# Packed attention values in one 128-column matmul per key chunk and head pair, in place of two of 64 columns

## The chip, the cores and the metric

The kernel runs on one core of one Trainium2 chip. The metric is the device time of one execution in microseconds (us). Three runs of the kernel before took 1108.59, 1109.92 and 1108.97 us, median 1108.97 us. A profile of one execution is read beside them.

TensorE is called PE below, and its loading of the stationary operand PEld; VectorE is DVE, ScalarE is ACT, GpSimd is POOL, and SyncE, which issues the transfers, is SP.

## The reference

Four batches, eight heads, 576 tokens, head dimension 64, 32 packed queries `p` per head. Two attentions follow each other, and two feed-forward stages follow them:

```python
def sm_attn(qq, kk, vv):
    s = scale * qq @ kk.T
    a = exp(s - max(s)); a = a / (sum(a) + 1e-9)
    return a @ vv
p_packed = sm_attn(p, k, v)            # 32 x 64 per head
out = sm_attn(q, p_packed, p_packed)   # 576 x 64 per head
# x: 2304 x 512; four experts of width 1024 with relu, weighted by domain_probs
# then h = x @ w_in (512 x 2048); g = h - tanh(h); g @ w_out
```

The change is in `a @ vv` of the first attention: 32 packed queries times 576 keys times 64 value columns, for 32 pairs of batch and head.

## The kernel before

The first attention is done per batch `b` and per half `g` of its eight heads. A half is two head pairs `jj`, a pair is two heads `h` whose value columns lie side by side. `pack_T(b, g)` transposes the softmax weights on PE into `a1t` (four chunks of 128 keys, for each of them 128 weight columns: two pairs, two heads, 32 queries) and `a1e` (the last 64 keys). `pack_pv(b, g)` multiplies them with the values: the value columns `vt` are the stationary operand, the weight columns stream. Per pair, per key chunk `c` (five, of which the last has 64 keys) and per head there is one matmul with 64 value columns and 32 weight columns. Head 0 writes PSUM partitions 0 to 63, head 1 partitions 64 to 127. The fp32 matmuls of this kind are two records each in the trace, a load and a stream each. At the end ACT copies the partitions 0 to 63 and DVE those from 64 to 127 into `ppbd`, block-diagonal, from which the second attention (`q_scores`, tile `qsc`) and the folded first expert weights (`pack_w1`, tile `wps`) read.

The order of the start is written out as a string of tokens. P is `pack_pv`, T is `pack_T`, M, E and N are the packed scores, their exponentials and their normalisation, Q, R and X are the scores, the normalisation and the transposes of the second attention, W is `pack_w1`, u and d are the expert's first and second matmuls (tiles `hps` and `yps`), f are filling matmuls on zeros (tile `warm`). `pack_pv` stands eight times there: P00 P01, one behind the other, in START_A, P02 and P03 in START_M, P10 to P13 in START_B. The two digits count groups of two batches and the four halves in each. PE runs in this written order from the start to the end of the expert stage. DVE and ACT follow it as far as START_M; in START_B and later the scheduler orders them by its own forecast, and by it the scheduler also chooses which of the four PSUM buffers of the pool `ps1` (tag p1: tp, te, pv, qsc, qtp, yps) a tile takes, and so whose release its first matmul waits for. The last stage (`h3ps`, `ops`) is ordered by the scheduler on all engines.

Of the kernel before, what the change touches and what calls it, by code (L numbers as in the profile page):

```python
# [8 lines left out]
F32 = mybir.dt.float32  # L9
F32R = mybir.dt.float32r  # L10
U32 = mybir.dt.uint32
ACTF = mybir.ActivationFunctionType
# [44 lines left out]
def kernel(  # L57
# [13 lines left out]
    nc = tc.nc  # L71
# [5 lines left out]
    def pool(name, bufs=1, stack=None, **kw):  # L77
        return (stack or ctx).enter_context(
            tc.tile_pool(name=name, bufs=bufs, **kw, **({} if kw.get('space') == DRAM else {'reuse_waits': 'tile'}))
        )  # L80
# [15 lines left out]
    ps1 = pool("ps1", 4, space=PSUM)  # L96
# [22 lines left out]
    ppbd, a2h, a2l = {}, {}, {}  # L119
# [7 lines left out]
    kv_k, kv_v, qs = {}, {}, {}  # L127
# [84 lines left out]
    def pack_pv(b, g):  # L212
        a1t, a1e = a1ts.pop((b, g))
        bi = b % 2
        pv = ps1.tile([128, 2, 32], F32, tag="p1", name="pv")
        for jj in range(2):
            j = 2 * g + jj
            for c in range(5):
                n = 128 if c < 4 else 64
                for h in range(2):  # L220
                    k0 = 64 * jj + 32 * h
                    nc.tensor.matmul(  # L222
                        out=pv[64 * h:64 * h + 64, jj, :],
                        lhsT=kv_v[b][c][0:n, 128 * j + 64 * h:128 * j + 64 * h + 64],
                        rhs=a1t[:, c, k0:k0 + 32] if c < 4 else a1e[0:64, k0:k0 + 32],
                        start=(c == 0), stop=(c == 4),
                    )
        js = slice(2 * g, 2 * g + 2)
        nc.scalar.activation(out=ppbd[b // 2][0:64, bi, js, 0:32], in_=pv[0:64], func=ACTF.Copy)
        nc.vector.tensor_copy(out=ppbd[b // 2][64:128, bi, js, 32:64], in_=pv[64:128])  # L230

    def q_scores(p, t0):
        nt = min(2, TP - t0)
# [249 lines left out]
    def late_norm():  # L483
# [8 lines left out]
        "R": lambda p, i: q_norm(p, 2 * i),  # L492
        "T": lambda p, i: pack_T(2 * p + i // 2, i % 2),
        "P": lambda p, i: pack_pv(2 * p + i // 2, i % 2),
        "Z": pp_split,
        "I": pp_init,
# [243 lines left out]
```

## Time and profile before

| what | value |
|---|---|
| three runs | 1108.59, 1109.92, 1108.97 us, median 1108.97 |
| profiled execution, its own time | 1108.61 us |
| its span, first to last instruction | 1106.8 us |
| granted clock of TensorE over the span | 1.00, the level of 2.4 GHz |
| PE busy | 1095.2 us, 99% of the span |
| PE records of `pack_pv` | 320 loads and 320 streams, between 12.6 and 84.5 us |

The page gives busy times and the chain of waits that ended last. The timeline gives starts. A PE record's duration is modelled and overlaps the next one, so what a matmul costs is read from one start to the next. The clock was 1.00 in every stretch that is used here.

### The profile page before, as it was taken

Reading aid. Unit: us, or ns where it says so; the run is one execution under the profiler, and the core shown is the slowest. Engines: PE = TensorE matmul, PEld = TensorE weight load, DVE = VectorE, ACT = ScalarE, POOL = GpSimd, SP = SyncE. Lnnn points to the kernel's source line nnn. Section 1 sums busy time; section 2 is a strip of 40 time slices with the busy share of each in tenths; the row PEclk is TensorE's granted clock in tenths of the full one; section 3 lists DMA queues with packets and bytes.
Section 4 is the critical chain, followed back from the end, with each engine's and each line's share of the span. In section 5 each row is a group of like instructions: output and inputs, shape, how many; then the busy total and the mean of one; then the engine's idle time right before and its main releaser. Section 6 shows DMA issues by size and latency. Waiting matters only on the chain.

```text
span 1106.8 us, 15428 instructions
## 1 busy us (share of the span) xinstructions
PE 1095.2 (99%) x6476; PEld 915.9 (83%) x6476; DVE 711.3 (64%) x960; ACT 468.5 (42%) x661; POOL 7.2 (1%) x11
## 2 busy tenths in 40 slices
PE   8999999999999999999999999999999999999998
PEld 6787888898888888888888888888888888888887
DVE  4636446776676676676676434587676757777775
ACT  3434433232332332333233112466657656656463
POOL 0100000000000000000000000000000000000000
PEclk9999999999999999999999999999999999999999
DMA  9731113223232241241331040401001262202102
GB/s 332 238 89 40 38 41 113 93 82 111 96 115 94 78 151 65 89 141 69 95 115 57 20 153 1 152 1 38 9 30 39 86 219 95 77 1 76 63 14 77
DMA packets 33669, 96.72 MB, mean 87 GB/s; under 512 B 3776, under 2 KB 3776, under 8 KB 33600
## 3 DMA queue, kind: packets, MB, share of 16 engines
q1 hardware_dynamic: 33600, 95.73, 25.3%
q8 instruction: 51, 0.84, 0.3%
q14 instruction: 18, 0.15, 0.0%
HBM read 69.51 MB, written 26.21 MB: 86 GB/s over the span
## 4 chain that ended last, share of the span: by engine, by line
PE 97%; DVE 1%; ACT 1%; DMA 0%; issue 0%; DVEq 0%; SPq 0%; ACTq 0%
PE yps L412 36%; PE hps L386 18%; PE ops L652 18%; PE h3ps L596 18%; PE wps L361 3%; PE pv L222 1%; PE qsc L244 1%; PE xps L447 1%; PE sc L166 1%; DMA kt<-in_kT_dram 0%; PE qtp L283 0%; PE tp L204 0%; ACT a L180 0%; DVE mx L175 0%; DVE a L191 0%
## 5 line engine op out<-in xcount | busy, mean ns | idle before, releaser
L412 PE MATMUL yps<-w2h,hm 128*128 128x512 f32 x640 | 208.9, 394 | 0.0
L596 PE MATMUL h3ps<-xh,ws 128*128 128x512 f32 (+1 forms) x640 | 187.2, 369 | 0.0
L652 PE MATMUL ops<-ws,gh 128*128 128x512 f32 x576 | 178.4, 396 | 0.0
L412 PE MATMUL yps<-w2h,hu 128*128 128x512 f32 x512 | 166.6, 391 | 0.0
L423 DVE SCALAR_TENSOR_TENSOR x<-yps,pn,x 128x512 f32<-128x512 f32 x126 | 94.6, 751 | 100.4 <-PE yps L412 97.9
L386 PE MATMUL hps<-a2h,wph 128*128 128x256 f32 (+1 forms) x512 | 152.3, 297 | 1.8 <-DVE xl L453 0.9
L386 PE MATMUL hps<-a2h,wpl 128*128 128x256 f32 (+1 forms) x512 | 151.8, 297 | 0.7 <-DVE wpl L368 0.7
L386 PE MATMUL hps<-a2l,wph 128*128 128x256 f32 (+1 forms) x512 | 151.7, 296 | 0.3 <-DVE a2l L287 0.3
L412 PEld LDWEIGHTS yps<-w2h,hm 128*128 128x128 f32 x640 | 120.3, 188 | 37.1 <-issue 12.6
L596 PEld LDWEIGHTS h3ps<-xh,ws 128*128 128x128 f32 x640 | 116.5, 189 | 20.5
L652 PEld LDWEIGHTS ops<-ws,gh 128*128 128x128 f32 x576 | 107.7, 189 | 24.0 <-ACT gh L631 0.2
L412 PE MATMUL yps<-w2l,hm 128*128 128x512 f32 x320 | 125.2, 391 | 0.0
L596 PE MATMUL h3ps<-xl,ws 128*128 128x512 f32 (+1 forms) x320 | 117.9, 368 | 0.0
L412 PEld LDWEIGHTS yps<-w2h,hu 128*128 128x128 f32 x512 | 96.3, 188 | 20.2 <-PE wps L361 0.8
L652 PE MATMUL ops<-ws,gl 128*128 128x512 f32 x288 | 110.9, 395 | 0.0
L395 ACT ACTIVATE hu<-hps 128x512 fp32r<-128x512 f32 x64 | 38.3, 598 | 168.5 <-PE hps L386 168.4
L395 ACT ACTIVATE hm<-hps 128x640 fp32r<-128x640 f32 x64 | 45.1, 704 | 135.4 <-PE hps L386 135.4
L386 PEld LDWEIGHTS hps<-a2h,wph 128*128 128x128 f32 x512 | 97.1, 190 | 5.5 <-DVE xl L453 1.1
L412 PE MATMUL yps<-w2l,hu 128*128 128x512 f32 x256 | 100.1, 391 | 0.0
L386 PEld LDWEIGHTS hps<-a2l,wph 128*128 128x128 f32 x512 | 97.2, 190 | 2.8 <-DVE a2l L287 0.5
L386 PEld LDWEIGHTS hps<-a2h,wpl 128*128 128x128 f32 x512 | 97.1, 190 | 0.9 <-DVE wpl L368 0.9
L396 DVE SCALAR_TENSOR_TENSOR hm<-hps,hm 128x640 fp32r<-128x640 f32 x64 | 52.7, 824 | 58.2 <-ACT hm L395 57.3
(95 smaller groups left out, 1402.2 us busy)
## 6 DMA issues: line engine op xcount, KB each, us to landing
w1f<-in_w_dram SPq DMA_DIRECT2D x16, 512.0 KB, 5.0
st<-in_w_dram SPq DMA_DIRECT2D x16, 512.0 KB, 3.8
f<-in_win_dram SPq DMA_DIRECT2D x16, 512.0 KB, 3.5
f<-in_wout_dram SPq DMA_DIRECT2D x16, 512.0 KB, 3.5
win<-fo SPq DMA_DIRECT2D x16, 512.0 KB, 2.6
wout<-fo SPq DMA_DIRECT2D x16, 512.0 KB, 2.6
ws<-win SPq DMA_DIRECT2D x16, 512.0 KB, 4.9
ws<-wout SPq DMA_DIRECT2D x16, 512.0 KB, 5.4
```

What stands on the lines that cost most here:

```text
L166: nc.tensor.matmul(out=sc[64 * jj:64 * jj + 64, h, 0:288], lhsT=pbd[:, 4 * b + j, :], rhs=kv_k[b][j][:, 288 * h:288 * h + 288],)
L222: nc.tensor.matmul(out=pv[64 * h:64 * h + 64, jj, :], lhsT=kv_v[b][c][0:n, 128 * j + 64 * h:128 * j + 64 * h + 64], rhs=a1t[:, c, k0:k0 + ...
L244: nc.tensor.matmul(out=sc[r - r0:r - r0 + 64, 256 * i:256 * i + 256].rearrange("p (r j k) -> p r j k", r=2, j=4)[:, :, j, :], lhsT=qs[2 * ...
L361: nc.tensor.matmul(out=ps[32 * j:32 * j + 32, r, :], lhsT=ppbd[p][d, bi, j, 32 * r:32 * r + 32], rhs=w1f[c, j // 2][d, j % 2, :],)
L386: nc.tensor.matmul(out=ps[:, ff, 0:n], lhsT=a[c, p, bi][:, g, c0:c0 + 128], rhs=x[p][:, g, t0:t0 + n], start=(k == 0), stop=(k == 5),)
L395: last[1] = nc.scalar.activation(out=hi[:, :, d], in_=ps[:, :, 0:n], func=ACTF.Relu).ins
L396: last[0] = nc.vector.scalar_tensor_tensor(out=lo[:, :, d], in0=ps[:, :, 0:n], scalar=0.0, in1=f(hi[:, :, d]), op0=ALU.max, op1=ALU.subtra ...
L412: nc.tensor.matmul(out=ps, lhsT=a[:, ff, o:o + 128], rhs=w[c, fp][:, ff], start=(k == 0), stop=(k == 11),)
L423: last[0] = nc.vector.scalar_tensor_tensor(out=x2[tt], in0=ps, scalar=pn[:, tt, e:e + 1], in1=x2[tt], op0=ALU.mult, op1=ALU.add,).ins
L447: nc.tensor.transpose(ps[:, k, 128 * i:128 * i + 128], x2[t0 + i][:, c0:c0 + 128], ident)
L596: nc.tensor.matmul(out=ps[:, ff, 0:n], lhsT=w[:, wl, kd, :], rhs=x[:, kd, :], start=(k == 0), stop=(k == 11),)
L652: nc.tensor.matmul(out=ops[u][t], lhsT=a[ff][:, d], rhs=w[:, wl], start=(i == 0 and ff == 0 and k == 0), stop=(i == 3 and ff == 1 and k == 2),
```

## The change

Per pair and key chunk there is one matmul in place of two: all 128 value columns of the pair are stationary, and the 64 weight columns of both heads stream. The output is 128 partitions by 64 columns, of which the two diagonal blocks are what is wanted: head 0 in partitions 0 to 63 and columns 0 to 31, head 1 in partitions 64 to 127 and columns 32 to 63. The off-diagonal blocks are not read. Tile `pv` becomes twice as wide, and the two copies at the end read a column slice of it.

```diff
-        pv = ps1.tile([128, 2, 32], F32, tag="p1", name="pv")
+        pv = ps1.tile([128, 2, 64], F32, tag="p1", name="pv")
...
-                for h in range(2):
-                    k0 = 64 * jj + 32 * h
-                    nc.tensor.matmul(
-                        out=pv[64 * h:64 * h + 64, jj, :],
-                        lhsT=kv_v[b][c][0:n, 128 * j + 64 * h:128 * j + 64 * h + 64],
-                        rhs=a1t[:, c, k0:k0 + 32] if c < 4 else a1e[0:64, k0:k0 + 32],
-                        start=(c == 0), stop=(c == 4),
-                    )
+                k = slice(64 * jj, 64 * jj + 64)
+                nc.tensor.matmul(
+                    out=pv[:, jj, :],
+                    lhsT=kv_v[b][c][0:n, 128 * j:128 * j + 128],
+                    rhs=a1t[:, c, k] if c < 4 else a1e[0:64, k],
+                    start=(c == 0), stop=(c == 4),
+                )
...
-        nc.scalar.activation(out=ppbd[b // 2][0:64, bi, js, 0:32], in_=pv[0:64], func=ACTF.Copy)
-        nc.vector.tensor_copy(out=ppbd[b // 2][64:128, bi, js, 32:64], in_=pv[64:128])
+        nc.scalar.activation(out=ppbd[b // 2][0:64, bi, js, 0:32], in_=pv[0:64, :, 0:32], func=ACTF.Copy)
+        nc.vector.tensor_copy(out=ppbd[b // 2][64:128, bi, js, 32:64], in_=pv[64:128, :, 32:64])
```

The file is one line shorter: what was line 222 is 221 now, and later lines move up by one too.

On PE, at P01 (two pairs) and the first scores of the second attention behind it, before:

```order
L222 MATMUL pv<-a1t,vt 64x32 x8
L222 MATMUL pv<-a1e,vt 64x32 x2
L222 MATMUL pv<-a1t,vt 64x32 x8
L222 MATMUL pv<-a1e,vt 64x32 x2
L244 MATMUL qsc<-ppbd,qt 64x2x32 x32
```

and after:

```order
L221 MATMUL pv<-a1t,vt 128x64 x4
L221 MATMUL pv<-a1e,vt 128x64
L221 MATMUL pv<-a1t,vt 128x64 x4
L221 MATMUL pv<-a1e,vt 128x64
L243 MATMUL qsc<-ppbd,qt 64x2x32 x32
```

The place in the order is the same; ten matmuls of full width stand for twenty of half width. So it is at all eight calls.

On ACT in START_B, where Q04, Q03, S10 (a packed score with its softmax), X02 and d000, d001 stand in the written order, before:

```order
L260 ACTIVATE a_624<-a_624 128x512 [waits DVE_49]
L421 ACTIVATE x_683<-yps,pn 128x512 [waits DVE_49,PE_49,Activation_49]
L286 ACTIVATE a2h<-qtp 128x2x256 [waits PE_49]
L260 ACTIVATE a_696<-a_696 128x256 [waits DVE_49,Activation_49]
L260 ACTIVATE a_723<-a_723 128x512 [waits DMAHW5_49,DVE_49]
L180 ACTIVATE a_740,ss<-sc,nm 128x576 [waits DMAHW1_49,DVE_49]
```

and after:

```order
L259 ACTIVATE a_584<-a_584 128x512 [waits DVE_49]
L285 ACTIVATE a2h<-qtp 128x2x256 [waits PE_49]
L420 ACTIVATE x_643<-yps,pn 128x512 [waits DVE_49,Activation_49]
L180 ACTIVATE a_700,ss<-sc,nm 128x576 [waits DMAHW1_49,DVE_49]
L259 ACTIVATE a_656<-a_656 128x256 [waits DVE_49,Activation_49]
L259 ACTIVATE a_683<-a_683 128x512 [waits DMAHW5_49,DVE_49]
```

The copy of d000's result (`x<-yps`) now stands behind the copy of X02's transposes (`a2h<-qtp`), and the exponential of S10 ahead of the two of Q04 and Q03.

On DVE at the same place, before:

```order
L267 TENSOR_SCALAR qsm<-qsm 128x16 [waits DVE_49]
L270 RECIPROCAL qsm<-qsm 128x16 [waits DVE_49]
L271 TENSOR_TENSOR a_624<-a_624,qsm 128x512 [waits DVE_49]
L254 TENSOR_REDUCE qmx<-qsc 128x8 [waits PE_49]
L254 TENSOR_REDUCE qmx<-qsc 128x16 [waits PE_49]
L175 TENSOR_REDUCE mx<-sc 128x1 [waits PE_49]
L257 TENSOR_TENSOR a_696<-qsc,qmx 128x256 [waits DVE_49]
L257 TENSOR_TENSOR a_723<-qsc,qmx 128x512 [waits DMAHW5_49,DVE_49]
L177 TENSOR_SCALAR nm<-mx 128x1 [waits DVE_49]
L287 TENSOR_TENSOR a2l<-qtp,a2h 128x2x256 [waits Activation_49]
```

and after:

```order
L253 TENSOR_REDUCE qmx<-qsc 128x8 [waits PE_49]
L266 TENSOR_SCALAR qsm<-qsm 128x16 [waits DVE_49]
L269 RECIPROCAL qsm<-qsm 128x16 [waits DVE_49]
L253 TENSOR_REDUCE qmx<-qsc 128x16 [waits PE_49]
L270 TENSOR_TENSOR a_584<-a_584,qsm 128x512 [waits DVE_49]
L175 TENSOR_REDUCE mx<-sc 128x1 [waits PE_49]
L177 TENSOR_SCALAR nm<-mx 128x1 [waits DVE_49]
L286 TENSOR_TENSOR a2l<-qtp,a2h 128x2x256 [waits Activation_49]
L256 TENSOR_TENSOR a_656<-qsc,qmx 128x256
L256 TENSOR_TENSOR a_683<-qsc,qmx 128x512 [waits DMAHW5_49]
```

Both maxima of Q04 and Q03 now stand ahead of the normalisation of R02 (`a<-a,qsm`), which X02 transposes, and X02's remainder (`a2l`) ahead of the two subtractions. With this order d001's `yps` got another PSUM buffer. Its first matmul waited for ACT, for the copy of d000's result (`x<-yps`); now it waits for DVE, for `a2l<-qtp`, the last reader of X02's transposes. On PE, after:

```order
L282 MATMUL qtp<-ident,a_584 128x128 [waits DVE_49,PE_49,Activation_49]
L282 MATMUL qtp<-ident,a_584 128x128 x3
L411 MATMUL yps<-w2h,hu 128x512 [waits DVE_49]
```

X02's four transposes and d001's first matmul follow each other on PE in both kernels; only what the last row waits for has changed. The last stage is shuffled too on PE, ACT and DVE, with the same instructions.

## Rows read from the trace of the kernel before

**Rows 1.** The page's first part: busy us (share of the span), instructions.

```profile
PE 1095.2 (99%) x6476; PEld 915.9 (83%) x6476; DVE 711.3 (64%) x960; ACT 468.5 (42%) x661; POOL 7.2 (1%) x11
```

**Rows 2.** Windows: stretch, us, busy PE, PEld, DVE, ACT, POOL, clock, DMA.

```profile
36.00:106.00 70.00, 69.96 (x726) 55.82 (x725) 38.14 (x84) 28.05 (x54) 2.35 (x1) 1.00 0.40 128
...
720.00:1060.00 340.00, 340.00 (x1547) 280.79 (x1546) 246.08 (x250) 206.72 (x254) 0.00 (x0) 1.00 0.18 61
```

**Rows 3.** Chain that ended last, to 180 us: start us, us, what.

```profile
12.69 3.32 PE pv L222 x80
...
82.92 1.65 PE pv L222 x40
```

**Rows 4.** Lines 222 and 481: operation, count, duration ns minimum/median/maximum, starts, forms.

```profile
L222 PEld LDWEIGHTS pv<-a1t,vt x256: 132/138/139, 12.6 to 84.1; 128*64 128x64 f32 x128
...
L481 PEld LDWEIGHTS warm<-blank x56: 186/192/334, 1.0 to 34.7; 128*128 128x128 f32 x56
```

**Rows 5.** Timeline of PE at P00 and P01: start us, us, what, count.

```profile
12.42 0.27 PE L205 MATMUL te<-ident,a 128*64 128x128 f32 x1
12.62 0.66 PE L222 MATMUL pv<-a1t,vt 128*64 128x32 f32 x16
...
15.91 0.45 PE L244 MATMUL qsc<-ppbd,qt 128*64 128x64 f32 x8
```

**Rows 6.** Timeline of PEld, P00's first pair and the next pair's start.

```profile
12.62 0.55 PEld L222 LDWEIGHTS pv<-a1t,vt 128*64 128x64 f32 x16 [0.20 <-issue]
13.21 0.19 PEld L222 LDWEIGHTS pv<-a1e,vt 64*64 64x64 f32 x4
13.44 0.55 PEld L222 LDWEIGHTS pv<-a1t,vt 128*64 128x64 f32 x16
```

**Rows 7.** Timeline of PEld: loads of 128 columns behind each other.

```profile
8.88 1.19 PEld L481 LDWEIGHTS warm<-blank 128*128 128x128 f32 x10 [0.44 <-issue]
...
54.61 0.19 PEld L412 LDWEIGHTS yps<-w2h,hm 128*128 128x128 f32 x1 [0.44 <-ACT a2h L286]
54.72 0.19 PEld L412 LDWEIGHTS yps<-w2l,hm 128*128 128x128 f32 x1
```

**Rows 8.** Timelines of PE and PEld: a transpose and filling matmuls behind it.

```profile
34.41 0.27 PE L205 MATMUL te<-ident,a 128*64 128x128 f32 x1
...
34.41 0.53 PEld L481 LDWEIGHTS warm<-blank 128*128 128x128 f32 x4
```

**Rows 9.** Timeline of PE ahead of P13.

```profile
82.30 0.39 PE L412 MATMUL yps<-w2l,hm 128*128 128x512 f32 x1
82.53 0.39 PE L412 MATMUL yps<-w2h,hm 128*128 128x512 f32 x1
82.85 0.54 PE L222 MATMUL pv<-a1t,vt 128*64 128x32 f32 x12
```

**Rows 10.** Timeline of PE behind P02: X01's transposes, T03, P03.

```profile
32.07 0.66 PE L283 MATMUL qtp<-ident,a 128*128 128x128 f32 x4
...
33.95 0.63 PE L204 MATMUL tp<-ident,a 128*128 128x128 f32 x4 [1.22 <-DVE a L191]
...
35.26 0.66 PE L222 MATMUL pv<-a1t,vt 128*64 128x32 f32 x16
```

**Rows 11.** Timeline of all engines around X02 and d001.

```profile
44.26 0.69 DVE L271 TENSOR_TENSOR a<-a,qsm 128x512 f32<-128x512 f32 x1
44.87 1.01 DVE L254 TENSOR_REDUCE qmx<-qsc 128x8 f32<-128x256 f32 x2
...
45.98 0.66 PE L283 MATMUL qtp<-ident,a 128*128 128x128 f32 x4
...
46.39 0.48 PE L412 MATMUL yps<-w2h,hu 128*128 128x512 f32 x1
...
46.67 0.60 ACT L286 ACTIVATE a2h<-qtp 128x512 fp32r<-128x512 f32 x1 [2.01 <-PE qtp L283]
...
47.75 0.68 DVE L287 TENSOR_TENSOR a2l<-qtp,a2h 128x512 fp32r<-128x512 f32 x1
```

## The prediction

> **What bounds the kernel now.** I read the page's first part: PE is busy 99% of the span [rows 1]. So what matters is PE's own time, and where PE still waits. The windows say that it waits almost nowhere: from 36 to 106 us it is busy for 69.96 of 70.00 us, in the last stage for 340.00 of 340.00 [rows 2]. The chain of waits that ended last shows where the eight calls of `pack_pv` lie on the way to the end: the pieces named pv begin with P00 and P01, 3.32 us, and end with P13, 1.65 us [rows 3]; between them stand P03, P10, P11 and P12 with 1.72, 1.65, 1.65 and 1.65 us. Seven of eight calls are on the chain. P02 alone is not, since PE sits idle for 1.22 us behind it [rows 10]. So 14 of the 16 head pairs cost what they take, in full, and nothing behind P03 absorbs it.
>
> **What a pair costs before.** The timeline of PE gives four pairs from 12.62 to 15.91 us [rows 5]: 0.823 us each. The loads show what is inside [rows 6]. Sixteen loads of the four full chunks take 0.55 us with a last one of 0.138 [rows 4]: the two heads load and stream side by side, in opposite halves of the array, and a step of such two is (0.55 - 0.138) / 7 = 0.059 us. There are ten steps per pair, because each fp32 matmul is two records. From the last step of the full chunks (12.62 + 0.55 - 0.138 = 13.03) to the first load of the chunk of 64 keys at 13.21 [rows 6] it is 0.18 us, and from its last step (13.21 + 0.19 - 0.131 = 13.27) back to 128 rows at 13.44 it is 0.17. Each change of shape thus costs some 0.11 to 0.12 us beyond a step, during which the array runs empty.
>
> So half of the records go, but they ran two at a time. The count of matmuls is no measure of the gain; the length of a step is.
>
> **What a pair costs after.** A step is now one load of 128 columns and one stream of 64. The nearest rows for the load: two loads of 128 columns behind each other, with nothing to stream in between, start at 54.61 and 54.72; ten filling loads take 1.19 us with a last one of 0.192, (1.19 - 0.192) / 9 = 0.111 [rows 7]. The durations agree: 192 ns for 128 columns and 138 for 64 [rows 4], 54 ns more for 64 columns more. I take 0.110 per step. The stream does not matter: the filling matmuls stream 128 columns in 0.111 [rows 7], so 64 need at most 0.056 and lie under the next load.
>
> The Trainium skill says the same of the load ("TensorE: Matmul & The Clock Gate", LDWEIGHTS): its time goes by the columns, columns over 1.2 in ns, so 107 ns for 128 and 53 for 64, whatever the rows. This speaks against the change, and the 54 ns between the two durations [rows 4] agree; by the page's 107 the sum below would be 14 x 8 x 0.003 = 0.3 us lower.
>
> The change between 128 and 64 rows stays, as the fifth chunk still has 64 keys. Its waits grow by the longer load (0.054) and the longer stream (at most 0.056 / 2 = 0.028) that must run out first: 0.18 + 0.08 = 0.26 and 0.17 + 0.08 = 0.25. A pair then takes 7 x 0.110 + 0.26 + 0.110 + 0.25 = 1.39 us, 0.567 more than before. Over 14 pairs on the chain that is **+7.9 us**. A 64-row matmul at full width does not occur before, so this has a lower bound: if it causes no emptying at all, ten steps of 0.110 make 1.10 us, 0.28 more per pair, +3.9 us.
>
> **What is saved at the entry.** Transposes and `yps` run at full width. Before, pv begins 0.20 us after the last transpose starts (12.42 to 12.62, rows 5) since the array must run empty; when filling matmuls of full width follow, their first load starts together with that transpose, at 34.41 [rows 8]. So the pv load moves up by 0.20 us at P00, P10, P11 and P12. At P13 `yps` is ahead: its step is 0.23 (82.30 to 82.53), and pv starts 0.32 behind the last one [rows 9]; after, the first load hides under that stream and the second starts at 0.23 in place of 0.32 + 0.11, again 0.20. Five times 0.20: **-1.0 us**.
>
> **P02.** Its two pairs grow by 1.13 us, and it gets a change of shape at its entry (half-width scores stand ahead), 0.12: 1.25 later in all. X01's transposes start at 33.32 in place of 32.07 [rows 10]. By the same chain at X02 [rows 11], ACT's copy starts 0.69 behind them and takes 0.60, DVE's remainder takes 0.68: done at 35.3. P03 waits for that buffer; it started at 35.26. T03, which waited for DVE until 33.95, is still ready in time [rows 10]. So the gap of 1.22 hides nearly all: **+0.2 us**, between 0 and 1.25 if nothing hides it.
>
> **The copies** at the end read as many elements as before, and behind P00 and P01 they follow the last matmul as before: nothing.
>
> **The new wait.** The scheduler gives d001's `yps` the buffer of X02's transposes. PE then stands, with all that is queued behind d001 on it (u001, X04 and so on), until ACT has copied them and DVE has taken the remainder. Before, d001 started right behind them, at 46.39. ACT's copy starts at 46.67 and takes 0.60; DVE's remainder comes behind nm alone now and no longer behind two subtractions, so it starts at about 47.29 and not at 47.75, and takes 0.68: 47.97 [rows 11]. That is **+1.6 us**, and no engine's lead can shorten it, since the transposes themselves start the chain. The normalisation that X02 needs ended at 44.95; with both maxima (1.01 us) ahead of it, it ends at about 45.96, and X02 started at 45.98 [rows 11]: **+0.1**, up to 0.7 if the later maximum waits for its scores.
>
> The shuffle of the last stage I cost at nothing: PE has work queued through all of it [rows 2], and the instructions are the same. If that cover is gone, a wait of a DVE row or two shows, under 1 us.
>
> **Sum**: 7.9 - 1.0 + 0.2 + 1.6 + 0.1 = +8.8 us, on the profiled execution's 1108.61: 1117.4. The median of the runs lies 0.36 above that execution, so 1117.8 against it; I say **1117.6**.
>
> **The rivals.** (a) *No emptying for the chunk of 64 keys.* Both ways of the change between 128 and 64 rows are in rows 6, at half width; at full width none is in the trace. If it is free there: 3.9 - 1.0 + 0.2 + 1.7 = +4.8, 1113.4 us. Against it: rows alone changed in rows 6, the width did not.
>
> (b) *Not slower: the load does not set the step.* If 0.059 is what any step takes, whatever its columns, ten steps and two changes of shape make a pair of the old 0.82 us; left are the entries (-1.0), the new wait (+1.7) and P02 (+0.2): +0.9, 1109.5 us. With (a) on top a pair falls to 0.59, 14 x -0.23 = -3.3, and the time to 1106.2. It decides from a step of about 0.068 us downwards, where 14 x 10 x 0.009 added to the 0.9 make 2.2 us. For it: streams of 32 columns are far shorter than 0.059, so the step could be a fixed cost of issue. Against it: the loads at 54.61 and 54.72 [rows 7] have nothing to wait for but the load ahead.
>
> The Trainium skill has a rule that would bring (b) about ("TensorE: Matmul & The Clock Gate", Back-to-back issue gap): up to 64 streamed columns the gap is about 60 cycles, a floor of some 25 ns, whatever is loaded. The same section says that loads and matmuls together set the spacing, and the 0.110 of rows 7 fits that.
>
> (c) *The new wait does not show*, because the buffer is free in time after all: 8.8 - 1.7 = +7.1, 1115.7 us. Against it: the chain of rows 11 starts with X02 itself.
>
> **How the numbers follow.** Forecast 70%, (a) 10%, (b) 5% with some 1109.5 and 2% with 1106.2, (c) 13%. A measurement of this kernel can tell 0.2%, 2.2 us, from no change. Slower by more: forecast, (a) and (c), 0.93, less 0.01 for what I have overlooked; within: 0.05; faster: 0.03. The range reaches down to (a), 1113.2, and up by the upper bounds: P02 with 1.0 more, X02 with 0.6 more, steps of 0.112 with 0.25 more, together 1119.5; I write 1119.8.
>
> **What would show it.** The timeline after should have pv records at steps of 0.11 us, pairs of 1.39, 0.11 from the last transpose to the first pv; on the chain P00 and P01 with about 5.4 us. At d001, PE should stand some 1.6 us and name DVE `a2l`. P03 should start within 0.5 us of where the shift of P00 and P01 alone puts it. If pv steps are 0.06, the load argument is wrong; if the fifth chunk follows at 0.11, the argument on emptying is.

## The result and the profile after

The changed kernel takes 1118.49 us (median of four runs, 1118.03 to 1119.71), the kernel before beside it 1109.45: ratio 1.0082, 95% interval 1.0070 to 1.0094. The forecast was 1117.6, slower: right in direction, and 0.9 us low. The profiled execution shows one term that the sum did not have.

Its own time is 1118.94 us, its span 1117.0 against 1106.8, so +10.2. The first part of the page (span; busy time, share and instructions of each engine):

```profile
span 1117.0 us, 15107 instructions
PE 1105.3 (99%) x6316; PEld 925.1 (83%) x6316; DVE 711.7 (64%) x960; ACT 468.6 (42%) x661; POOL 7.2 (1%) x11
```

PE has fewer instructions than in [rows 1], and is still busy 99% of a longer span. The chain of waits that ended last (start, length, what) answers to [rows 3]:

```profile
12.44 5.41 PE pv L221 x40
...
32.49 2.79 PE pv L221 x20
...
37.37 2.83 PE pv L221 x20
...
49.17 0.64 PE qtp L282 x4
49.84 0.61 ACT a2h L285
50.47 0.70 DVE a2l L286
...
51.21 4.61 PE yps L411 x12
...
71.58 2.60 PE pv L221 x20
```

P00 and P01 went from 3.32 to 5.41 us with half the records, P10 from 1.65 to 2.60. New on the chain are P02 and, from 49.17 us, the new wait: X02's transposes, ACT's copy, DVE's remainder, then d001.

The timeline of the weight loads answers to [rows 6]:

```profile
12.17 0.97 PEld L221 LDWEIGHTS pv<-a1t,vt 128*128 128x128 f32 x8
13.21 0.29 PEld L221 LDWEIGHTS pv<-a1e,vt 64*128 64x128 f32 x2
13.57 0.97 PEld L221 LDWEIGHTS pv<-a1t,vt 128*128 128x128 f32 x8
```

Eight loads in 0.97 us, the last of them 0.19 long, make a step of (0.97 - 0.19) / 7 = 0.111 us. A pair takes 13.57 - 12.17 = 1.40 us. The last transpose starts at 12.17 as well, so pv's first load no longer comes 0.20 us behind it.

The timeline of PE at d001 (in brackets: time stood before the instruction, and for what), to be held against [rows 11]:

```profile
49.17 0.63 PE L282 MATMUL qtp<-ident,a 128*128 128x128 f32 x4 [0.46 <-DVE a L270]
51.21 0.67 PE L411 MATMUL yps<-w2h,hu 128*128 128x512 f32 x1 [1.42 <-DVE a2l L286]
51.68 0.63 PE L411 MATMUL yps<-w2l,hu 128*128 128x512 f32 x1
52.11 1.05 PE L411 MATMUL yps<-w2h,hu 128*128 128x512 f32 x2
...
55.66 0.30 PE L385 MATMUL hps<-a2h,wph 128*128 128x320 f32 x1
```

PE stands 1.42 us for `a2l`, as forecast. But the matmuls behind it then come at steps of 0.43 us (51.68 to 52.11) where `yps` otherwise steps at 0.23 [rows 9]. The windows of the same stretch say why (busy time of PE, PEld, DVE, ACT and POOL; then the granted clock of TensorE, the DMA share, GB/s):

```profile
50.00:51.20 1.20, 0.00 (x0) 0.00 (x0) 0.73 (x2) 1.20 (x3) 0.00 (x0) 1.00 1.04 400
51.20:52.00 0.80, 0.79 (x2) 0.70 (x3) 0.80 (x2) 0.80 (x3) 0.00 (x0) 0.61 1.06 405
52.00:53.00 1.00, 1.00 (x4) 0.71 (x4) 0.96 (x5) 0.67 (x2) 0.00 (x0) 0.50 1.07 346
...
55.00:56.00 1.00, 1.00 (x7) 0.86 (x6) 0.22 (x1) 0.14 (x1) 0.00 (x0) 1.00 1.07 383
```

The granted clock is 0.50, the 1.2 GHz level, from about 51.4 us for some 3.4 us. d001 takes 55.66 - 51.21 = 4.45 us, up to the start of u001 (`hps`). Before, it took 49.22 - 46.39 = 2.83: it began at 46.39 [rows 11], and u001 followed in the timeline of PE:

```profile
49.22 0.30 PE L386 MATMUL hps<-a2h,wph 128*128 128x320 f32 x1
```

The whole difference, followed by the start of the same work in the timelines of PE of both traces:

| work on PE | before | after | shift | added since the row above | forecast |
|---|---|---|---|---|---|
| last transpose ahead of P00 | 12.42 | 12.17 | -0.25 | -0.25 (first loads landed earlier) | 0 |
| `qsc` behind P01 | 15.91 | 17.76 | +1.85 | +2.10 | +2.07 |
| P03 (so P02's price) | 35.26 | 37.37 | +2.11 | +0.26 | +0.2 |
| `wps` behind P03 | 36.91 | 40.14 | +3.23 | +1.12 | +1.13 |
| X02's transposes | 45.98 | 49.17 | +3.19 | -0.04 | +0.1 |
| d001 | 46.39 | 51.21 | +4.82 | +1.63 | +1.6 |
| u001 | 49.22 | 55.66 | +6.44 | **+1.62** | **0** |
| `yps` behind P13 | 84.49 | 94.72 | +10.23 | +3.79 | +3.74 |
| end of the span | 1106.8 | 1117.0 | +10.2 | 0.0 | 0 |

Every term of the sum is met within 0.15 us. The 0.25 us at the start is no term of it: this execution's first loads landed earlier. One term was missing: the clock. Nothing is gained or lost behind P13, so the last stage hides its shuffle.

### The profile page after: what moved, and what is told of

The parts are those of the page before. It is cut to its first block, busy times and chain, and to the rows that moved or that the text cites. A ratio compares the mean times of both kernels' runs of the same rounds, so it can differ in the third digit from the quotient of the medians.

```text
span 1117.0 us, 15107 instructions
## 1 busy us (share of the span) xinstructions
PE 1105.3 (99%) x6316; PEld 925.1 (83%) x6316; DVE 711.7 (64%) x960; ACT 468.6 (42%) x661; POOL 7.2 (1%) x11
## 4 chain that ended last, share of the span: by engine, by line
PE 97%; DVE 2%; ACT 1%; issue 0%; DVEq 0%; ACTq 0%
PE yps L411 36%; PE hps L385 18%; PE ops L651 18%; PE h3ps L595 18%; PE wps L360 3%; PE pv L221 2%; PE sc L166 1%; PE xps L446 1%; PE qsc L243 1%; PE qtp L282 0%; PE warm L480 0%; DVE qmx L253 0%; DVE a2l L286 0%; PE tp L204 0%; ACT a L180 0%
```

## The experiments

Each was timed beside the kernel before. Ratios are given with their 95% interval. "Mean clock" is the granted clock averaged over a whole execution. It turns out to be the key to half of the results: no profiled execution with 0.999 or 1.0 has a low stretch before its last 2 us, and those with 0.998 have 3.4 us of it.

### Filling the pause at d001

```diff
-START_L = "... S10 X02 d001 "
+START_L = "... S10 X02 c6 d001 "
+    def cover(n):
+        t = ps2.tile([128, 2, 512], F32, tag="p2", name="cov")
+        for i in range(n):
+            nc.tensor.matmul(out=t[:, i % 2, 0:128], lhsT=blank, rhs=blank)
...
+        "c": cover,
```

> The changed kernel with six FP32 matmuls of 128 by 128 (operands all zero, result read by nobody) put on PE between X02 and d001; the wait of d001 for DVE's a2l stays. Each filler should take about 0.23 us at full clock (two records of 0.11), so six fill the 1.4 us in which PE stood. Theory 'the pause lets the clock fall': the granted clock stays at 1.0 between 51 and 55 us, d001 takes 2.7 to 3.0 us in place of 4.6, and the kernel ends 1.4 to 1.8 us before the changed one (about 9.0 - 1.6 = +7.4 us on the kernel before, ratio 1.0067). Rival 'the slow steps come from d001's own operands or from traffic beside it': d001 keeps 4.6 us with the granted clock at 1.0 or 0.5, and the time stays at +9.0 (1.0082) or a little above.

Measured: 1119.01 us, 1.0083 (1.0070 to 1.0097), no gain where 1.0067 was expected. Still d001 ran at full clock, 52.65 to 55.50, 2.85 us. The windows show where the gain went:

```profile
14.00:18.00 4.00, 4.00 (x31) 3.60 (x30) 0.23 (x1) 0.22 (x1) 0.00 (x0) 1.00 1.06 402
18.00:19.00 1.00, 1.00 (x11) 0.88 (x10) 0.15 (x1) 0.22 (x1) 0.00 (x0) 0.56 0.98 389
19.00:20.00 1.00, 1.00 (x20) 0.87 (x18) 0.08 (x1) 0.00 (x0) 0.00 (x0) 0.50 1.04 397
...
21.00:22.00 1.00, 1.00 (x28) 0.93 (x25) 0.97 (x2) 0.00 (x0) 0.00 (x0) 0.73 1.06 348
...
51.00:56.00 5.00, 4.93 (x31) 4.24 (x29) 4.31 (x16) 3.13 (x7) 0.00 (x0) 1.00 1.06 348
```

The clock fell all the same, from 18.1 to 21.5 us, at the end of P01. By the records' modelled durations PE had then been busy for 4.00 of 4.00 us. All four runs had a mean clock of 0.997 or 0.998, like all four of the changed kernel. So a fall does not need the pause at d001. My first theory, and the rival beside it, were both about the wrong place.

### Taking the wait away

```diff
-START_L = "... d000 Q04 R04 Q03 R03 S10 X02 d001 "
+START_L = "... d000 Q04 Q03 M10 X02 E10 R04 R03 N10 d001 "
-    with tc.manual_schedule(engines={mybir.EngineType.SP}):
+    with tc.manual_schedule(engines=rest):
         run(START_L)
```

> The changed kernel with the late part of the start recorded in another order (M10, X02, E10, R04, R03, N10 in place of R04, R03, S10, X02) and with DVE's and ACT's order taken from it, so that d001's result tile gets a buffer whose last readers are long done, not X02's. Theory 'shifted buffer, then clock': PE no longer stands 1.4 us at d001, the granted clock stays at 1.0 there, d001 takes about 2.75 us, and the time falls by both, 1.6 + 1.6 = 3.2 us: about +5.8 us on the kernel before (1.0052). Rival 'the wait is only moved': another wait of 1 us or more stands in X02, d001 or u001, and less than 1.5 us is gained (1.0070 or more).

Measured: 1119.13 us, 1.0081 (1.0067 to 1.0094), mean clock 0.997, 0.997, 0.997, 0.998. The timeline of PE at X02 and d001, and the windows:

```profile
52.11 0.66 PE L282 MATMUL qtp<-ident,a 128*128 128x128 f32 x4
52.52 0.47 PE L411 MATMUL yps<-w2h,hu 128*128 128x512 f32 x1
```

```profile
18.00:21.00 3.00, 3.00 (x31) 2.63 (x32) 0.23 (x1) 0.22 (x1) 0.00 (x0) 0.50 1.02 401
21.00:24.00 3.00, 3.00 (x49) 2.88 (x46) 1.93 (x3) 0.63 (x1) 0.00 (x0) 0.50 1.06 313
24.00:25.00 1.00, 1.00 (x8) 1.00 (x7) 0.97 (x3) 0.09 (x1) 0.00 (x0) 0.62 1.03 303
```

The time is not the 1.0052 that was expected. At its place the theory is right: d001 starts 0.41 us behind X02, without a wait, and takes 55.37 - 52.52 = 2.85 us. But this execution was at half clock from about 18.0 to 24.8 us, which costs half of that, 3.4 us, the whole gain. Its first transposes also came 1.06 us later. By time alone the rival ("the wait is only moved") would have won; no moved wait is in the trace. What the wait is worth had to be priced in a kernel whose clock stays up (below).

> Control: the same reordering of the start in the kernel before, where d001 waits for nothing. Theory: no difference, within 0.6 us of the kernel before (0.9995 to 1.0005), so that what seq_after gains is the new wait and its clock, not the order. Rival: the order itself is worth something, 1 us or more either way.

Measured: 1110.27 us, 1.0010 (1.0001 to 1.0019). The order alone is not free for the kernel before, where no more than 1.0005 was expected: PE stands 0.68 us at 53 us, ahead of transposes of the scores (`qtp`), where it had not. It gives nothing in any case, so a gain of the changed kernel from this edit is the wait's.

### The same columns streamed under half-width loads

```diff
-        pv = ps1.tile([128, 2, 32], F32, tag="p1", name="pv")
+        pv = ps1.tile([128, 2, 64], F32, tag="p1", name="pv")
-                    k0 = 64 * jj + 32 * h
+                    k0 = 64 * jj
-                        rhs=a1t[:, c, k0:k0 + 32] if c < 4 else a1e[0:64, k0:k0 + 32],
+                        rhs=a1t[:, c, k0:k0 + 64] if c < 4 else a1e[0:64, k0:k0 + 64],
...
```

This is the kernel before; its two copies read a column slice, as in the changed kernel.

> The kernel before (two loads of 64 value columns per key chunk and pair, each head on its own half of the columns) with each load streaming all 64 weight columns of the pair in place of 32; the two foreign blocks are written and not read. The values' results are unchanged. Theory 'the load of the stationary columns sets the step': pairs stay at 0.82 to 0.85 us and pv costs nothing more; d001's result tile takes X02's buffer here too (64 columns make no difference to that), so the new wait and the low clock come alone, +3.2 us (ratio 1.0029). Rival 'the streamed columns set it': the pair rises to 1.2 to 1.4 us, 14 pairs add 5 to 8 us, and the whole is +8 to +11 us (1.0075 to 1.01).

Measured: 1111.54 us, 1.0015 (1.0006 to 1.0024), mean clock 0.999 or 1.0 in all eleven runs. The first loads of pv, and the timeline of PE (its third row holds only what starts before 13 us):

```profile
11.78 0.55 PEld L222 LDWEIGHTS pv<-a1t,vt 128*64 128x64 f32 x16 [0.20 <-issue]
```

```profile
11.78 0.69 PE L222 MATMUL pv<-a1t,vt 128*64 128x64 f32 x16
12.40 0.33 PE L222 MATMUL pv<-a1e,vt 64*64 64x64 f32 x4
12.66 0.51 PE L222 MATMUL pv<-a1t,vt 128*64 128x64 f32 x10
...
48.13 0.50 PE L412 MATMUL yps<-w2h,hu 128*128 128x512 f32 x1 [1.41 <-DVE a2l L287]
```

A pair takes 12.66 - 11.78 = 0.88 us: twice the columns cost 0.05 beside 0.82. The step is as in [rows 6], sixteen loads in 0.55 us. So at the same 64 streamed columns a step is 0.059 us under two loads of 64 side by side and 0.111 under one of 128: the width of the load sets it, and rival (b) of the prediction falls. The new wait is here in full, with half-width loads: it comes with the scheduler's choice of buffers (this kernel's pv tile has 64 columns a pair, as in the changed one), not with the full-width matmuls. And with the wait there is no fall of the clock:

```profile
48.00:56.00 8.00, 7.87 (x48) 6.95 (x50) 5.46 (x16) 4.28 (x9) 0.00 (x0) 1.00 0.91 298
```

I had expected +3.2 us, 1.6 of it for the clock. That half did not come.

### More and fewer columns under full-width loads

The two edits, first 128 columns, then 32. The second leaves out the block of the pair's second head:

```diff
-        pv = ps1.tile([128, 2, 64], F32, tag="p1", name="pv")
+        pv = ps1.tile([128, 2, 192], F32, tag="p1", name="pv")
+            o = pv.rearrange("p a b -> p (a b)")[:, 128 * jj:128 * jj + 128]
-                    out=pv[:, jj, :],
+                    out=o,
-                    rhs=a1t[:, c, k] if c < 4 else a1e[0:64, k],
+                    rhs=a1t[:, c, :] if c < 4 else a1e[0:64, :],
```

```diff
-                k = slice(64 * jj, 64 * jj + 64)
+                k = slice(64 * jj, 64 * jj + 32)
-                    out=pv[:, jj, :],
+                    out=pv[:, jj, 0:32],
...
-        nc.vector.tensor_copy(out=ppbd[b // 2][64:128, bi, js, 32:64], in_=pv[64:128, :, 32:64])
+        nc.vector.tensor_copy(out=ppbd[b // 2][64:128, bi, js, 32:64], in_=pv[64:128, :, 0:32])
```

> The changed kernel with every one of its full-width loads streaming 128 weight columns (both pairs of the entry) in place of 64; the foreign blocks are written and not read, the results are the same. Theory 'the load of 128 value columns sets the step': the step stays at 0.11 us and a pair at 1.40 us although twice as much is streamed; rival 'the stream sets it': the pair goes to 2 us or more, 16 pairs cost some 10 us more (ratio 1.017). On the clock, which fell for 3 to 7 us at differing places of the start in every run of the three full-width kernels so far (mean granted clock 0.997 to 0.998), and in none of the runs of the half-width kernel with 64 streamed columns (0.999 to 1.0): theory 'it falls because PE streams few columns per us in pv': with twice the columns the mean clock is 0.999 to 1.0 in all runs and the time about 1.6 us below the changed kernel's (1.0065); rival 'it falls because PE stands idle in the start': 0.997 to 0.998 as in the changed kernel, 1.008.

> The changed kernel with 32 weight columns streamed per load in place of 64: the second head's block of the pair is left out (its results take the first head's weights). Theory 'the load sets the step': 0.11 us and 1.40 us a pair, although half as much is streamed, time as the changed kernel's or a little above (1.008 to 1.010); rival 'the stream sets it': the pair falls to 0.8 to 1.1 us and the time by 4 to 8 us (1.001 to 1.005). On the clock, theory 'few streamed columns': mean clock 0.995 to 0.998 in all runs, none at 0.999 or above; rival 'idle time': the same 0.997 to 0.998, so this run alone does not part them.

Measured: 128 columns 1119.91 us, 1.0086 (1.0071 to 1.0101), mean clock 1.0, 1.0, 0.998, 0.998; 32 columns 1122.69 us, 1.0115 (1.0088 to 1.0143), mean clock 0.994, 0.991, 0.997, 0.992. The loads, of 128 columns first, then of 32:

```profile
11.87 0.97 PEld L221 LDWEIGHTS pv<-a1t,vt 128*128 128x128 f32 x8
...
13.38 0.97 PEld L221 LDWEIGHTS pv<-a1t,vt 128*128 128x128 f32 x8
```

```profile
12.63 0.97 PEld L221 LDWEIGHTS pv<-a1t,vt 128*128 128x128 f32 x8
...
13.98 0.97 PEld L221 LDWEIGHTS pv<-a1t,vt 128*128 128x128 f32 x8
```

Eight loads take 0.97 us whether 32, 64 or 128 columns are streamed: the load sets the step. Only the change of shape grows with the columns, so a pair takes 1.35, 1.40 and 1.51 us. That is why 128 columns are not faster although two of four runs kept their clock: 16 pairs at 0.11 are 1.8 us. On the clock neither forecast for 128 columns holds: it was to stay up in all runs, or in none.

With 32 columns the profiled execution has three low stretches. The first begins in P01, at 17.4 us, the second right behind P02, at 37.9, and the third behind the pause at d001, at 54.9; they make 13.6 us in all:

```profile
18.00:24.00 6.00, 6.00 (x74) 5.69 (x75) 3.21 (x6) 1.03 (x3) 0.00 (x0) 0.50 1.03 350
...
38.00:41.00 3.00, 3.00 (x17) 2.83 (x15) 1.09 (x3) 2.15 (x4) 0.00 (x0) 0.50 0.50 173
...
55.00:58.00 3.00, 3.00 (x8) 2.34 (x7) 2.93 (x12) 0.92 (x2) 0.00 (x0) 0.50 1.06 312
```

### The keys cut without a chunk of 64

The same edit in both kernels (here in the changed one, in part; the loads of v, the copies and the operands are cut to match):

```diff
-        tp = ps1.tile([128, 4, 128], F32, tag="p1", name="tp")
-        te = ps1.tile([128, 128], F32, tag="p1", name="te")
+        tp = ps1.tile([128, 3, 128], F32, tag="p1", name="tp")
+        te = ps1.tile([128, 2, 128], F32, tag="p1", name="te")
...
-        nc.tensor.transpose(te[0:64, :], a1[:, 512:576], ident)
+        for c in range(2):
+            nc.tensor.transpose(te[0:96, c, :], a1[:, 384 + 96 * c:480 + 96 * c], ident)
...
-                n = 128 if c < 4 else 64
+                n = 128 if c < 3 else 96
```

> The kernel before with the 576 keys cut into chunks of 128, 128, 128, 96 and 96 in place of four of 128 and one of 64, so that no load uses a 64-row shape. Theory 'a change of the load's shape empties PE': the pair falls from 0.82 us to about 0.59 us (ten steps of 0.059), 14 pairs on the path give 3.3 us: ratio 0.997. Rival 'the time at the change belongs to the 64-row loads or to the accumulation's end': the pair stays within 0.05 us of 0.82, ratio 1.000.

> The changed kernel with the same cut of the keys, 128, 128, 128, 96, 96. Theory 'a change of shape empties PE': the pair falls from 1.40 to about 1.12 us (ten steps of 0.112), 14 to 16 pairs on the path give 3.9 to 4.4 us less than the changed kernel, ratio about 1.0045; the new wait at d001 stays. Rival: the pair stays within 0.05 us of 1.40, ratio 1.008.

Measured: in the kernel before 1107.53 us, 0.9977 (0.9968 to 0.9986), **faster than both kernels of this study**; in the changed kernel 1114.28 us, 1.0038 (1.0025 to 1.0051). The loads of the kernel before with the new cut, then of the changed one with it:

```profile
12.69 0.43 PEld L222 LDWEIGHTS pv<-a1t,vt 128*64 128x64 f32 x12 [0.18 <-issue]
13.04 0.32 PEld L222 LDWEIGHTS pv<-a1e,vt 96*64 96x64 f32 x8
13.27 0.44 PEld L222 LDWEIGHTS pv<-a1t,vt 128*64 128x64 f32 x12
```

```profile
12.96 0.75 PEld L221 LDWEIGHTS pv<-a1t,vt 128*128 128x128 f32 x6
13.63 0.53 PEld L221 LDWEIGHTS pv<-a1e,vt 96*128 96x128 f32 x4
14.08 0.75 PEld L221 LDWEIGHTS pv<-a1t,vt 128*128 128x128 f32 x6
```

Pairs take 0.58 and 1.12 us, ten steps each and nothing else: what the prediction calls emptying, the time lost at the chunk of 64 keys, is real at both widths, 0.24 and 0.28 us a pair. So the prediction's rival (a), that it is free at full width, falls too. A whole call of the kernel before saves less than two such pairs. On its chain P10 to P13 now take 1.29 us each, where they took 1.65 [rows 3], so 0.36 a call:

```profile
66.66 1.29 PE pv L222 x40
```

The last pair of such a call is only some 0.12 us shorter. The changed kernel gained 4.5 us of span, not for the reason alone that I gave. X02 starts only 0.73 us earlier, since the first transposes of that execution came 0.79 later, and 0.48 us of standing at T03 and a longer S10 took most of the rest; 8 pairs behind it give 2.2; the last 1.6 is the clock, which stayed at 0.999 to 1.0 in all five runs with the new wait in place. The timeline of PE and the window of that stretch:

```profile
50.51 0.50 PE L411 MATMUL yps<-w2h,hu 128*128 128x512 f32 x1 [1.41 <-DVE a2l L286]
```

```profile
50.00:58.00 8.00, 7.49 (x46) 6.73 (x48) 5.46 (x16) 4.29 (x10) 0.00 (x0) 1.00 0.99 300
```

### The wait's price, and the clock once more

The last three combine edits shown above: the new cut with the reordered start; the new cut with 32 columns; and, in the kernel before, the new cut, 64 columns and the reordered start.

> The changed kernel with the keys cut 128, 128, 128, 96, 96 (its granted clock stayed at 0.999 to 1.0 in all five runs) and with the reordered start that gives d001 a free buffer. It prices the wait of d001 with the clock out of the way. Theory 'the wait is on the path': 1.4 to 1.9 us less than the kernel with the new cut alone (1114.3 us, ratio 1.0038), that is 1.0021 to 1.0026, PE not standing at d001, clock 0.999 to 1.0. Rival 'the wait hides another one': less than 0.7 us gained, 1.0032 or more, with another wait of 1 us or more between X02 and u001.

Measured: 1112.51 us, 1.0024 (1.0016 to 1.0033), mean clock 0.999 or 1.0 in eleven runs. The timeline of PE:

```profile
47.82 0.66 PE L282 MATMUL qtp<-ident,a 128*128 128x128 f32 x4
48.23 0.48 PE L411 MATMUL yps<-w2h,hu 128*128 128x512 f32 x1
```

d001 starts 0.41 us behind X02, where it starts 2.07 behind it with the new cut alone (48.44 to 50.51 us), so 1.66 us are gained at the place itself. The median is 1.8 us lower (by the ratios, each against its own runs of before, 0.0014 or 1.6 us, with intervals that just overlap). So the wait is worth its 1.6 us once the clock doesn't move.

> The changed kernel with the keys cut 128, 128, 128, 96, 96 and 32 weight columns streamed per load in place of 64: the second head's block of the pair is left out. The load still sets the step, so a pair stays at 1.12 us. On the clock: the new cut alone kept it at 0.999 to 1.0 in five runs of five although PE stood 1.4 us at d001. Theory 'few streamed columns per us let it fall': mean clock 0.998 or lower in all runs or all but one, time 1.5 to 5 us above 1114.3 (ratio 1.005 to 1.008). Rival 'the 64-row loads or the emptying around them let it fall': 0.999 to 1.0 again, ratio 1.0035 to 1.0045.

Measured: 1116.38 us, 1.0065 (1.0042 to 1.0088), mean clock 0.991 to 0.998 in six runs of six. Here the stretch at half clock begins in P01, at 15.9 us, and lasts until 22.7; none lies behind the pause at d001:

```profile
16.00:19.00 3.00, 3.00 (x24) 2.81 (x24) 0.23 (x1) 0.22 (x1) 0.00 (x0) 0.50 1.04 406
...
50.00:58.00 8.00, 6.59 (x37) 5.41 (x36) 5.59 (x16) 4.18 (x8) 0.00 (x0) 1.00 1.06 328
```

> The kernel before with three edits together: keys cut 128, 128, 128, 96, 96, each half-width load streaming all 64 weight columns, and the reordered start (so that d001 waits for nothing). Theory 'more streamed columns hold the clock': mean clock 0.999 to 1.0 in all runs, where the new cut alone had 0.996 or 0.997 in three of ten; a pair takes 0.62 to 0.65 us against 0.59, 0.5 to 0.8 us over 14 pairs, so the median is about that of the new cut alone (1107.5, ratio 0.9975 to 0.9985) with a smaller spread. Rival 'the clock's fall has nothing to do with it': 0.996 to 0.998 in three or more of ten runs and the median 0.5 to 1 us higher, 0.998 to 0.999.

Measured: 1107.73 us, 0.9982 (0.9973 to 0.9990), mean clock 0.999 or 1.0 in eleven of eleven, spread 1106.49 to 1108.62. A pair takes 0.58 us as with 32 columns, where 0.62 to 0.65 was expected: without a change of shape, twice the columns are free. The median still doesn't fall below that of the new cut alone; the reordered start has waits of its own (PE stands 0.51 us at 44 and 0.56 at 53 us).

The clock over all runs of the experiments and the four of the changed kernel ("fall" below: a mean clock of 0.998 or less):

| kernel | load | columns per load | cut | pair, us | runs with mean clock of 0.998 or less |
|---|---|---|---|---|---|
| before | 64 | 32 | old | 0.82 | 23 of 58 |
| before, reordered | 64 | 32 | old | 0.82 | 4 of 11 |
| before, 64 columns | 64 | 64 | old | 0.88 | 0 of 11 |
| before, new cut | 64 | 32 | new | 0.58 | 3 of 10 |
| the same, 64 columns, reordered | 64 | 64 | new | 0.58 | 0 of 11 |
| changed, 32 columns | 128 | 32 | old | 1.35 | 4 of 4 (down to 0.991) |
| changed (as it is, filled, reordered) | 128 | 64 | old | 1.40 | 12 of 12 |
| changed, 128 columns | 128 | 128 | old | 1.51 | 2 of 4 |
| changed, new cut, 32 columns | 128 | 32 | new | 1.12 | 6 of 6 |
| changed, new cut (as it is, reordered) | 128 | 64 | new | 1.12 | 0 of 16 |

Where kernels differ in the streamed columns (one of them in the order, another in the new wait too), more columns went with fewer falls or shallower ones: 0 of 16 against 6 of 6 at the bottom. The cut of the keys did as much: with 64 columns under full-width loads 12 of 12 runs fall with the old cut and none of 16 with the new one. The pause at d001 doesn't order them: kernels with it are at 0 of 11 and 0 of 5, one without it (reordered) at 4 of 4.

Standing is not out of it, though. The profiles hold eight low stretches. Five begin in pv or right behind it while PE is busy. Three begin 0.2 to 0.5 us after a stand of 1.4 to 1.6 us: at d001 in the changed kernel and in the one with 32 columns, and behind P02, from 34.2 us on, in the kernel before with the new cut. What sets off a fall, and why the kernel before falls in 23 of 58 runs while the changed one under the new cut, whose pairs are longer, falls in none, stays open. The stand behind P02 [rows 10] is not enough by itself: the kernels with 64 columns under half-width loads have it too, 1.11 and 1.55 us, and no fall in 22 runs.

## Why the prediction was right, and what it missed

**Step, emptying, entry.** Right, each by its sign. Forecast were 0.110, pairs of 1.39 and 0.20 saved at the entry; the trace has 0.111, 1.40 and 0.20. All eight calls of pv together cost 7.3 us on the chain, P02 included, against 7.9 - 1.0 + 0.2 = 7.1. Both rivals that priced them otherwise were tried and fall: (b) by the 0.97 us of eight full-width loads at 32, 64 and 128 columns, against 0.55 for sixteen of half width at 64, and (a) by the 0.28 us that the cut without a chunk of 64 took from a pair.

The Trainium skill ("TensorE: Matmul & The Clock Gate", Back-to-back issue gap) had the rule by which (b) would have come about, a small gap for up to 64 streamed columns. Here 32 streamed columns stand at 0.111 us a record under 128-column loads, so the load decides. LDWEIGHTS on the same page of the Trainium skill prices a load of 128 columns at 128 / 1.2 = 107 ns; the trace has 111.

**P02** cost 0.26 where 0.2 was forecast. **X02** was forecast at +0.1 and came out at 0.0: it does stand 0.46 us for the normalisation, but S10 ahead of it is 0.5 us shorter, presumably as its keys have landed by then. Two errors of the same size hide each other, which is luck; the bound of 0.7 was nearer to the wait itself.

**The new wait** was 1.63 for 1.6. Rival (c) falls by the timeline, and by the 1.66 us that d001 comes closer to X02 in the kernel with the new cut when the buffer is free.

**What it missed: the clock.** The step that failed is one that the prediction takes without saying it: that d001, once started, runs as before. I costed the wait as time stood and took every duration behind it, and behind the small matmuls of pv, from rows at full clock. In the profiled execution this left out 1.62 us. The kernel before falls too in 23 of 58 runs, which are 1.6 us longer (medians 1110.8 and 1109.2); the execution I built on had no fall. So the changed kernel turns a cost that two runs in five had into one that every timed run has. The forecast of the median lay 0.9 us low. That it lay no lower is in part luck: the profiled execution before was the fastest of its four runs, while the one after lies 0.45 us above its median, and so the profiled spans differ by 10.2 us and the medians by 9.0 only.

The Trainium skill (same page, What's actually happening) ties the clock to how busy PE has been, with idleness as what lowers it, and says that the number of slow matmuls differs from run to run. The second agrees: the mean clock of the kernel before goes from 1.0 down to 0.995 over its 58 runs. The first fits only in part. In the kernel with the filled pause PE had been busy for 4.00 of 4.00 us, by modelled durations, when the clock fell, and 1.41 us of standing lowered nothing in the kernel with 64 columns under half-width loads. At the same full-width loads two things turned falls on or off here: the number of streamed columns, and the cut of the keys. Why they do is not shown.

## What to carry to other kernels

Price a small matmul by the longer of its load and its stream: joining two half-width column tiles that ran side by side into one full-width load halves the records and not the time, since a step went from 0.059 to 0.111 us. Look for the changes of shape instead: cutting 576 keys as 128, 128, 128, 96, 96 in place of four of 128 and one of 64 took 0.24 us from a pair that another one follows, 0.36 from a call of two, and made the kernel before 0.23% faster. And list the mean granted clock of every run before believing a difference of 1 or 2 us in a kernel with stretches of small matmuls: two edits that did what they should at their place (filling a pause, freeing a buffer) showed nothing in the time because the clock fell elsewhere.

## What the runs showed of the hardware that was not expected

- The granted clock fell to 0.5 while PE was busy for all of the time by modelled durations, in pv under full-width loads: low stretches of 3.4 to 6.8 us, at differing places from kernel to kernel, three in one execution when only 32 columns were streamed per load.
- Kernels that fill the streams with columns that nobody reads kept the clock: 64 in place of 32 under half-width loads, 0 falls in 11 runs against 23 in 58, at 0.05 us a pair with the old cut; with the new cut 0 in 11 against 3 in 10, at no cost in a pair (0.58 us both).
- The time lost at a change between 128 and 64 rows grows with the streamed columns: pairs of 1.35, 1.40 and 1.51 us with 32, 64 and 128 columns, at the same step of 0.111.
- A load of 96 rows steps like one of 128, in 0.111 us at 128 columns and 0.058 for two side by side at 64, and the change between 128 and 96 rows costs nothing that the trace shows.
